# Attention ahead of a gated FFN: the queries of the first eight steps without their zeros, scored head by head on tiles of 64 rows by 32 columns, in a new order of all work

## The chip, the cores and the metric

The kernel runs on one core of a Trainium2 chip. The metric is the device time of one execution in microseconds (us); lower is better. Before the change it was 360.17 us, the median of three runs (359.59, 360.17 and 361.05).

## What is computed

Four batches, eight heads, 768 positions, 64 elements a head. The positions are cut into 24 chunks of 32. A chunk's queries see 16 positions to the left, their own 32, 8 to the right, and 8 memory positions that each head has of its own. The result goes through a feed-forward layer with a convolution over three positions and a sigmoid gate:

```
for c in range(nc):                                   # 24 chunks of 32 positions
    k_full = concat(mem_k, k[l_start:r_end])          # 8 memory + up to 56 positions
    scores = 1/sqrt(64) * q_c @ k_full.T
    a = exp(scores - max(scores));  a = a / (sum(a) + 1e-09)
    out[c] = a @ v_full
x = out, heads side by side                           # 4 x 768 x 512
h = relu(x @ w_in)                                    # 512 -> 1024
conv = w[0] * h[t-1] + w[1] * h[t] + w[2] * h[t+1]
y = (h * sigmoid(conv)) @ w_out                       # 1024 -> 512
```

All inputs are float32 except the three weights of the FFN, which are float64.

## The kernel before

**Steps.** Attention is cut into 32 steps. A step is one batch, one half of the positions (`hf`, 12 chunks) and one pair of heads (`cc`, 0 to 3). A step loads three tiles through SyncE's queue: the queries `q_d` (128 partitions by 12 x 64, 384 KB), the keys and memory keys `k_t` (128 by 504, 252 KB) and the values `v_t` (128 by 768, 384 KB). Steps 0 to 3 keep queries and keys in buffers named `h`, steps 4 to 7 in buffers named `g`, which the FFN uses later; the others use two buffers each of `q_d` and `k_t`.

In `q_d` the partitions are 2 heads x 64 elements. For each chunk there are 64 columns: the first 32 hold head 0's queries in partitions 0 to 63 and zeros below, the last 32 hold head 1's queries in partitions 64 to 127 and zeros above (`_laid_out` writes this on the host as it lays the inputs out). So half of what is loaded is zeros, and one matmul with all 128 rows gives the scores of both heads of a chunk.

**Scores (`scores`, L476 to L490).** Twelve matmuls, one for each chunk, each 64 queries by 64 keys, in the two column halves of the array (`j`). All land in one PSUM bank `s` (a ring of two banks). The trace shows two records for each such float32 matmul, 24 for a step.

**Softmax.** VectorE takes the maximum (L398), subtracts it (L403), ScalarE takes the exponential (L436); or ScalarE does both from PSUM (L424) with the maximum as its bias, with (`B`) or without (`A`) the sums. Then sums (L449), 1e-9 (L453), reciprocal (L456) and the product (L460) on VectorE or GpSimd. The strings `SOFT`, `ZADD` and `NORM` choose engine and form for each step.

**Outcome.** Three transposes on TensorE (L506), two copies to `a_d` on ScalarE (L517), twelve matmuls with the values (L525), then `x_hi` on ScalarE (L534) and `x_lo` on VectorE (L537): two parts of the attention output for the FFN. Transposes and values share a ring of two PSUM banks, `ta`.

**FFN.** `w_in` and `w_out` come as float64 and are split into a high and a low part by `from_f64`; the letters of `W_IN` and `W_OUT` choose the engines of the eight pieces of each (`c` and `C` use ScalarE and GpSimd for some operations, `R` and `S` use GpSimd for three or two, `M` nearly only VectorE; a small letter puts L294 on GpSimd). `ffn_in` (L560) takes twelve matmuls of 384 columns for a piece of 128 hidden channels and half the positions; `gate` and `split` do convolution, sigmoid and product on VectorE, ScalarE and GpSimd (`TAP`, `MULT`, `LO`); `ffn_out` (L636) takes 24 matmuls for 128 positions.

**Order.** Nothing is scheduled by hand. `Plan` takes every operation with an engine, a cost and a due time, and places them in one list: on each engine the ready operation with the smallest due time is next. `DUE` holds the due times as start and step of a line for each stage, `SWITCH` and `MODE` are added to the due time where ScalarE's table or TensorE's tiling would change. The list sets the order of the instructions of every engine and of the DMA queue. On the chip the engines wait for each other by semaphores only.

Of the kernel before, what the change touches and what calls it, by code (L numbers as in the profile page):

```python
# [19 lines left out]
CH, LEFT, RIGHT, NMEM = 32, 16, 8, 8  # L20
KW = LEFT + CH + RIGHT + NMEM
STEP = CH + NMEM
NH = 2
NC = 12
NG = NC // 4
KC = STEP * (NC - 1) + KW

TINY = 1.75 * 2.0**-15
W64 = 3
WC = 512  # L30


W_IN, W_OUT = "ccRRMMcR", "CCCsSRmm"

TAP = "AAAAAAAAAVAVVVVVVAAAAAVAAVVAAAVA"
MULT = "GGGGGGGGGGGGGVVGGGVVGGGGGGGVGVGG"
LO = "VVVGGGGGGGVVVGVVVVVVVVGGGGGGGVVG"
SOFT = "VVAVVVVVVVVVVVAABBVVVVVVBBVVVVBB"  # L40
NORM = "GGGGGGGGGGGGGGVGGGGVGVGVVVVVGGGV"
ZADD = "VGGGGVGGGVGVVGGGVVVVGGGVVVVGVVVV"
GROUP = "11111111"

DUE = {
    "early": (1.5, 1.76), "qk0": (-11, 1.21), "v0": (46.7, 0), "late": (-4.7, 0.51), "w_in": (-21.5, 2.2),
    "w_in_load": (-23.8, 6.98), "w_out": (61.7, 2.41), "w_out_load": (18.4, 7.34), "load": (-167, 1.78),
# [4 lines left out]
    "gate": (1.2, 6.13)  # L52
}
# [9 lines left out]
class Plan:  # L63
# [47 lines left out]
    def run(self):  # L111
        ops = self.ops
        n = len(ops)
# [21 lines left out]
        for _ in range(n):  # L135
# [34 lines left out]
            t, e, i = best  # L170
            eng, cost, due, do, after, tiles, shared, tab, md, late = ops[i]
# [3 lines left out]
            if md and md != mode:  # L175
                cost += 95 if md == "tiled" else 200
                mode = md
# [35 lines left out]
PAIRS = False  # L213
SWITCH, MODE = 102.0, 16.4


@with_exitstack
def attention_then_gated_ffn(
    ctx: ExitStack,
    tc: tile.TileContext,  # L220
    q: bass.AP,
    k: bass.AP,
# [150 lines left out]
    def attention(steps, due, soft, norm, zadd):  # L373
# [9 lines left out]
        for i, n in enumerate(steps):  # L383
            b, r = divmod(n, NU)
            cc = r % NCC

            q_d, k_t = (tile_of(*(("h", NFC) if n < 4 else ("g", 2 * NFC) if n < 8 else (x, 2)), y) for x, y in (("q_d", [P, NC, 2 * CH]), ("k_t", [P, KC])))
            v_of[n] = v_t = tile_of("v_t", 3, [P, NG, 2, 2, D])
            s = bank("s", 2)
            qk, vd = (lin("qk0", n), lin("v0", n)) if n < 8 else (due[i] - DUE["load"][0], due[i] - DUE["load"][0] + DUE["load"][1])  # L390
            load(q_d, q[b, hf, cc], qk, "p c q -> p (c q)")
            load(k_t, k[b, hf, cc], qk)
            load(v_t, v[b, hf, cc], vd, "p g c h d -> p (g c h d)")
            scores(s, q_d, k_t, due[i])
            s_ = lambda s=s: s.t[:, :W].rearrange("p (g k) -> p g k", k=KW)
# [79 lines left out]
    def scores(s, q_d, k_t, due):  # L475
# [257 lines left out]
def _laid_out(q, k, v, mem_k, mem_v):  # L733
# [22 lines left out]
    for h in range(2):  # L756
        ql[:, :, :, h, :, :, h] = qt[:, :, :, h]
    ql = ql.reshape(B, NH, H // 2, 2 * D, NC * 2 * CH)
    w = windows(k, mem_k).reshape(B, H // 2, 2, NH, NC, KW, D)
    kl = np.empty((B, H // 2, 2, NH, KC, D), k.dtype)  # L760
# [4 lines left out]
    vl = w.transpose(0, 3, 1, 6, 7, 4, 5, 2, 8).reshape(B, NH, H // 2, 2 * KW, NG * 4 * D)  # L765
    return [np.ascontiguousarray(a) for a in (ql, kl, vl)]

# [39 lines left out]
```

## Time and profile before

| | |
|---|---|
| median of three runs | 360.17 us |
| the profiled execution's own time | 359.69 us |
| its span, first to last instruction | 357.8 us |
| VectorE busy | 248.4 us (69%) |
| ScalarE busy | 231.6 us (65%) |
| GpSimd busy | 152.5 us (43%) |
| moved by DMA | 48.62 MB |

The span is what the profile's times refer to; 1.9 us of the execution lie around it. Engines are named PE (TensorE's matmuls), PEld (its weight loads, which overlap the matmuls), DVE (VectorE), ACT (ScalarE), POOL (GpSimd) and SP (SyncE, which only issues DMAs). A line of a timeline gives start, duration, engine, source line, the operation with what it writes and reads, the number of instructions, and in brackets the idle time of the engine before it with what ended it.

### The profile page before, as it was taken

Reading aid. Unit: us, or ns where it says so; the run is one execution under the profiler, and the core shown is the slowest. Engines: PE = TensorE matmul, PEld = TensorE weight load, DVE = VectorE, ACT = ScalarE, POOL = GpSimd, SP = SyncE. Lnnn points to the kernel's source line nnn. Section 1 sums busy time; section 2 is a strip of 40 time slices with the busy share of each in tenths; the row PEclk is TensorE's granted clock in tenths of the full one; section 3 lists DMA queues with packets and bytes.
Section 4 is the critical chain, followed back from the end, with each engine's and each line's share of the span. In section 5 each row is a group of like instructions: output and inputs, shape, how many; then the busy total and the mean of one; then the engine's idle time right before and its main releaser. Section 6 shows DMA issues by size and latency. Waiting matters only on the chain.

```text
span 357.8 us, 7562 instructions
## 1 busy us (share of the span) xinstructions
PE 339.2 (95%) x3000; PEld 301.3 (84%) x3000; DVE 248.4 (69%) x401; ACT 231.6 (65%) x457; POOL 152.5 (43%) x180
## 2 busy tenths in 40 slices
PE   1789999999999998998999999999999999999996
PEld 1678898989999876876888899999878799998886
DVE  2798998999999699998994026998503137998000
ACT  3568777579898898769734137999837345764201
POOL 5356616544783589676321003015721005783200
PEclk9999999999999999999999999999999999999999
DMA  7999892768451047480401200461312100000111
GB/s 286 401 393 330 279 333 82 276 209 266 163 177 61 0 147 235 163 289 35 178 2 59 88 31 0 147 235 27 136 64 71 61 29 2 0 0 2 59 59 60
DMA packets 19907, 48.62 MB, mean 136 GB/s; under 512 B 2336, under 2 KB 6688, under 8 KB 19872
## 3 DMA queue, kind: packets, MB, share of 16 engines
q1 hardware_dynamic: 19872, 48.14, 38.4%
q8 instruction: 24, 0.39, 0.5%
q14 instruction: 11, 0.09, 0.1%
HBM read 41.84 MB, written 6.29 MB: 135 GB/s over the span
## 4 chain that ended last, share of the span: by engine, by line
PE 61%; DVE 20%; DMA 8%; ACT 5%; issue 3%; POOL 2%; SPq 0%; ACTq 0%
PE f L636 29%; PE f L560 26%; PE ta L525 3%; DVE c L597 2%; DVE w_top L307 2%; DVE z L449 2%; DMA v_t<-in_v_dram 2%; DMA g<-in_q_dram 2%; PE s L482 2%; DVE x_lo L537 2%; DMA h<-in_k_dram 2%; DVE w L328 1%; DVE w_top L300 1%; DMA w<-in_w_in_dram 1%; DVE w L321 1%
## 5 line engine op out<-in xcount | busy, mean ns | idle before, releaser
L636 PE MATMUL f<-w_out_hi,g 128*128 128x512 f32 (+1 forms) x400 | 126.6, 390 | 0.0
L560 PE MATMUL f<-x_hi,w_in_hi 128*128 128x384 f32 x256 | 88.2, 344 | 0.0
L636 PEld LDWEIGHTS f<-w_out_hi,g 128*128 128x128 f32 x400 | 74.0, 188 | 16.5 <-POOL g L618 0.4
L560 PE MATMUL f<-x_lo,w_in_hi 128*128 128x384 f32 x256 | 86.3, 337 | 0.6 <-DVE x_lo L537 0.6
L560 PE MATMUL f<-x_hi,w_in_lo 128*128 128x384 f32 x256 | 86.1, 336 | 0.0
L636 PE MATMUL f<-w_out_lo,g 128*128 128x512 f32 (+1 forms) x200 | 77.1, 386 | 0.0
L597 DVE SCALAR_TENSOR_TENSOR c<-h,cw,c 128x768 f32<-128x768 f32 x48 | 66.9, 1399 | 11.3 <-ACT c L587 9.6
L560 PEld LDWEIGHTS f<-x_hi,w_in_hi 128*128 128x128 f32 x256 | 48.1, 188 | 1.1 <-ACT g L577 0.3
L560 PEld LDWEIGHTS f<-x_lo,w_in_hi 128*128 128x128 f32 x256 | 48.1, 188 | 1.1 <-DVE x_lo L537 1.1
L560 PEld LDWEIGHTS f<-x_hi,w_in_lo 128*128 128x128 f32 x256 | 48.2, 188 | 0.2
L605 POOL TENSOR_TENSOR c<-c,h 128x768 f32<-128x768 f32 x12 | 21.4, 1785 | 61.7 <-ACT c L601 61.6
L636 PEld LDWEIGHTS f<-w_out_lo,g 128*128 128x128 f32 x200 | 37.6, 188 | 7.2
L648 ACT COPY o_sb<-f 128x512 f32<-128x512 f32 (+1 forms) x25 | 14.0, 569 | 40.9 <-PE f L636 33.6
L460 POOL TENSOR_TENSOR e<-e,z 128x384 f32<-128x384 f32 x23 | 22.7, 988 | 32.1 <-DVE e L444 12.9
L577 ACT ACTIVATE h<-f 128x384 f32<-128x384 f32 x48 | 23.1, 491 | 19.3 <-PE f L560 19.0
L517 ACT COPY a_d<-ta 64x384 f32<-64x384 f32 x64 | 30.2, 472 | 7.2 <-PE ta L506 6.4
L601 ACT ACTIVATE c<-c 128x768 f32<-128x768 f32 x32 | 26.9, 846 | 9.5 <-DVE c L597 7.2
L537 DVE TENSOR_TENSOR x_lo<-ta,x_hi 128x384 fp32r<-128x384 f32 x32 | 16.9, 545 | 22.6 <-ACT x_hi L534 22.2
L618 POOL TENSOR_TENSOR g<-c,g 128x768 fp32r<-128x768 f32 x13 | 28.6, 2213 | 7.9 <-ACT g L615 7.9
L525 PEld LDWEIGHTS ta<-a_d,v_t 128*64 128x64 f32 x768 | 24.4, 138 | 5.6 <-issue 2.8
L525 PE MATMUL ta<-a_d,v_t 128*64 128x64 f32 x768 | 27.3, 224 | 1.3 <-DMA v_t<-in_v_dram 1.2
L615 ACT CAST g<-c 128x768 fp32r<-128x768 f32 x24 | 19.9, 828 | 6.4 <-POOL c L605 4.9
(76 smaller groups left out, 488.4 us busy)
## 6 DMA issues: line engine op xcount, KB each, us to landing
v_t<-in_v_dram SPq DMA_DIRECT2D x32, 384.0 KB, 4.7
q_d<-in_q_dram SPq DMA_DIRECT2D x24, 384.0 KB, 4.8
k_t<-in_k_dram SPq DMA_DIRECT2D x24, 252.0 KB, 4.9
out_dram<-o_sb SPq DMA_DIRECT2D x23, 256.0 KB, 2.0
w<-in_w_in_dram SPq DMA_DIRECT2D x8, 512.0 KB, 5.1
w<-in_w_out_dram SPq DMA_DIRECT2D x8, 512.0 KB, 3.9
h<-in_q_dram SPq DMA_DIRECT2D x4, 384.0 KB, 7.2
g<-in_q_dram SPq DMA_DIRECT2D x4, 384.0 KB, 6.6
```

What stands on the lines that cost most here:

```text
L460: lambda i=i: (nc.vector if norm == "V" else nc.gpsimd).tensor_tensor(out=part(e, i), in0=part(e, i), in1=part(z, i).unsqueeze(2).broadcas ...
L517: nc.scalar.copy(out=a_d[r, :, p, :], in_=t.t[r, : NG * P].rearrange("p (g q) -> p g q", q=CH))
L525: nc.tensor.matmul(a.t[h * D : (h + 1) * D, g * P + j * D : g * P + (j + 1) * D], lhsT=v_t.t[:, g, j, h], rhs=a_d[:, 4 * g + 2 * j + h].re ...
L537: lambda: nc.vector.tensor_tensor(out=x_lo.t[:, cc], in0=a.t[:, :TW], in1=x_hi.t[:, cc].bitcast(F32), op=ALU.subtract),
L560: nc.tensor.matmul(f.t[:, :TW], lhsT=w_in_p[c][:, fc, cc], rhs=x_p[a].t[:, cc], start=(cc == 0 and i == 0), stop=(cc == NCC - 1 and i == 2),)
L577: nc.scalar.activation(h.t[:, 1 + o : 1 + o + TW], f.t[:, :TW], AF.Relu)
L597: lambda i=i: nc.vector.scalar_tensor_tensor(out=c.t, in0=h.t[:, i : i + S], scalar=w[i], in1=c.t, op0=ALU.mult, op1=ALU.add), (*H, c), (c ...
L601: plan.op("A", act(S), due, lambda: nc.scalar.activation(c.t, c.t, AF.Sigmoid), (c,), (c,), table="sigmoid")
L605: lambda: (nc.vector if mult == "V" else nc.gpsimd).tensor_tensor(out=y(), in0=c.t, in1=h.t[:, 1 : S + 1], op=ALU.mult), (c, h), (h if kee ...
L615: plan.op("A", act(S), due, lambda: nc.scalar.copy(out=g_hi(), in_=x()), (h,), (p[0],))
L618: lambda: (nc.vector if lo == "V" else nc.gpsimd).tensor_tensor(out=g_lo(), in0=x(), in1=g_hi().bitcast(F32), op=ALU.subtract), (h, p[0]), ...
L636: nc.tensor.matmul(ps.t[:, :n], lhsT=g[fc][a].t[:, tt * P : (tt + 1) * P], rhs=w_out_p[c][:, fc, o : o + n], start=(fc == 0 and i == 0), s ...
```

## The change

A new input `q_first` holds the queries of the first eight steps without zeros: 128 partitions (2 heads x 64) by 12 chunks x 32 queries, 192 KB a step in place of 384 KB. Their scores are taken by a new function, `scores_apart`: for each chunk and head one matmul with the 64 rows of that head and 32 columns, so 24 matmuls for a step in place of 12. The four that follow each other (`j`, `h`) go to the four 32-partition quarters of the same PSUM bank, and what they write is what `scores` wrote. The planner counts them as a third tiling mode. Steps 8 to 31 keep their form.

The letters of all engine strings, all due times, `SWITCH` and `MODE`, and the planner's cost for a change of tiling are new as well; `SOFT` for instance gives step 2 the form `B` in place of `A`.

```diff
+NQ = 8
-W_IN, W_OUT = "ccRRMMcR", "CCCsSRmm"
+W_IN, W_OUT = "SRRRSCRC", "sSCsRRRm"
-MULT = "GGGGGGGGGGGGGVVGGGVVGGGGGGGVGVGG"
+MULT = "GGGGGVVVVGGVGVVVVGGVVVVGGGGGGVVV"
...
-    "early": (1.5, 1.76), "qk0": (-11, 1.21), "v0": (46.7, 0), "late": (-4.7, 0.51), "w_in": (-21.5, 2.2),
+    "early": (1.5, 3.25), "qk0": (-19.9, 1.15), "v0": (21.1, 0), "late": (-15.5, 0.53), "w_in": (-7.3, 2.44),
...
-                cost += 95 if md == "tiled" else 200
+                cost += 95 if mode == "whole" else 200 if md == "whole" else 140
...
-("q_d", [P, NC, 2 * CH])
+("q_d", [P, NC, CH if n < NQ else 2 * CH])
-            load(q_d, q[b, hf, cc], qk, "p c q -> p (c q)")
+            load(q_d, q_first[n] if n < NQ else q[b, hf, cc], qk, "p c q -> p (c q)")
-            scores(s, q_d, k_t, due[i])
+            (scores_apart if n < NQ else scores)(s, q_d, k_t, due[i])
...
+    def scores_apart(s, q_d, k_t, due):
+        def mm():
+            for g in range(NG):
+                for p in range(2):
+                    for j in range(2):
+                        for h in range(2):
+                            c, r, o = 4 * g + 2 * j + p, slice(h * D, (h + 1) * D), (2 * g + p) * KW
+                            nc.tensor.matmul(
+                                s.t[j * D + h * CH : j * D + (h + 1) * CH, o : o + KW],
+                                lhsT=q_d.t[r, c],
+                                rhs=k_t.t[r, c * STEP : c * STEP + KW],
+                                start=True,
+                                stop=True,
+                            )
+        plan.op("PE", 48 * 16, due, mm, (q_d, k_t), (s,), mode="rows", late=250)
```

**TensorE, from its first matmul to the first matmul of the FFN.** Before (`s` are scores, `ta` transposes and values; twelve matmuls are one step's scores or values, three are one step's transposes):

```order
L482 MATMUL s<-h 64x64 x48
L506 MATMUL ta<-ident,e 128x128 x3
L482 MATMUL s<-g 64x64 x12
L506 MATMUL ta<-ident,e 128x128 x3
L482 MATMUL s<-g 64x64 x24
L525 MATMUL ta<-a_d_71,v_t 64x64 x12
L525 MATMUL ta<-a_d_72,v_t 64x64 x12
L560 MATMUL f<-x_hi_337,w_in_hi 128x384
```

The same place in the changed kernel, where 24 matmuls of 32 by 64 are one step's scores (L503), L527 the transposes, L546 the values and L581 the FFN:

```order
L503 MATMUL s<-h 32x64 x96
L527 MATMUL ta<-ident,e 128x128 x6
L503 MATMUL s<-g 32x64 x48
L546 MATMUL ta<-a_d_71,v_t 64x64 x12
L503 MATMUL s<-g 32x64 x24
L546 MATMUL ta<-a_d_72,v_t 64x64 x12
L581 MATMUL f<-x_hi_406,w_in_hi 128x384
```

Both transposes now stand ahead of step 4's scores, and step 6's scores stand between the two groups of values. Seven steps' scores are ahead of the FFN in both.

**SyncE's DMA queue, from its start.** Before:

```order
L287 DMA w_82<-in_w_in_dram 128x1024
L287 DMA w_84<-in_w_in_dram 128x1024
L472 DMA h<-in_q_dram 128x768
L472 DMA h<-in_k_dram 128x504
L287 DMA w_90<-in_w_in_dram 128x1024
L472 DMA h<-in_q_dram 128x768
```

and now:

```order
L289 DMA w_82<-in_w_in_dram 128x1024
L474 DMA h<-in_q_first_dram 128x384
L474 DMA h<-in_k_dram 128x504
L474 DMA h<-in_q_first_dram 128x384
L474 DMA h<-in_k_dram 128x504
L474 DMA h<-in_q_first_dram 128x384
```

One piece of `w_in` (512 KB) is ahead of step 0 in place of two. The second now stands behind step 3's keys and the third behind step 7's; then come three `v_t` in both kernels.

**VectorE, from its start to the reciprocal of step 0.** Before, with two pieces of `w_in` (`w_82`, `w_84`) between the steps' operations:

```order
L316 TENSOR_SCALAR w_82<-w_82 128x512
L321 SCALAR_TENSOR_TENSOR w_82<-w_82 128x512
L316 TENSOR_SCALAR w_84<-w_84 128x512
L300 TENSOR_SCALAR w_top<-w_top 128x512
L398 TENSOR_REDUCE top<-s 128x6
L403 TENSOR_TENSOR e<-s,top 128x384
L307 SCALAR_TENSOR_TENSOR w_top<-w_82,w_top 128x512
L328 TENSOR_SCALAR w_82<-w_top 128x512
```

and now:

```order
L296 TENSOR_SCALAR w_top<-w_top 128x512
L302 TENSOR_SCALAR w_top<-w_top 128x512
L309 SCALAR_TENSOR_TENSOR w_top<-w_82,w_top 128x512
L330 TENSOR_SCALAR w_82<-w_top 128x512
L400 TENSOR_REDUCE top<-s 128x6
L405 TENSOR_TENSOR e<-s,top 128x384
L400 TENSOR_REDUCE top<-s 128x6
L405 TENSOR_TENSOR e<-s,top 128x384
L343 SCALAR_TENSOR_TENSOR w_82<-w_82 128x512
```

Steps 0 and 1 have their maximum and difference one behind the other, and one operation on the weights stands between them and step 2's.

More of the change, by code (lines that the diff above doesn't have):

```diff
@@ L28 @@
 TINY = 1.75 * 2.0**-15
+NQ = 8
 W64 = 3
 WC = 512
-W_IN, W_OUT = "ccRRMMcR", "CCCsSRmm"
-TAP = "AAAAAAAAAVAVVVVVVAAAAAVAAVVAAAVA"
-MULT = "GGGGGGGGGGGGGVVGGGVVGGGGGGGVGVGG"
[L39 to L42, printed above, removed]
+W_IN, W_OUT = "SRRRSCRC", "sSCsRRRm"
+TAP = "AAAAAAAAVAVAAVAAVVAAAAAAAVAAVAVV"
+MULT = "GGGGGVVVVGGVGVVVVGGVVVVGGGGGGVVV"
+LO = "VGVGVGGGVGVGVVVVVGVVGGGGGVVGGVVV"
+SOFT = "VVBVVVVVBVVVVVAABBVVVVVVVVVAAVAV"
+NORM = "GGVGGGGGGGGGGGGVGGVVGGVVGGGGVGGG"
+ZADD = "VGGGGVGGVVVVGGGGGVGGGGVVGVVGGVVV"
 GROUP = "11111111"
 DUE = {
-    "early": (1.5, 1.76), "qk0": (-11, 1.21), "v0": (46.7, 0), "late": (-4.7, 0.51), "w_in": (-21.5, 2.2),
-    "w_in_load": (-23.8, 6.98), "w_out": (61.7, 2.41), "w_out_load": (18.4, 7.34), "load": (-167, 1.78),
[4 rows of a table removed]
-    "gate": (1.2, 6.13)
+    "early": (1.5, 3.25), "qk0": (-19.9, 1.15), "v0": (21.1, 0), "late": (-15.5, 0.53), "w_in": (-7.3, 2.44),
+    "w_in_load": (-23.6, 7.37), "w_out": (60.9, 2.74), "w_out_load": (25.4, 4.97), "load": (-219.2, 1.82),
[4 rows of a table added]
+    "gate": (-4.6, 9.82)
 }
@@ L213 @@
 PAIRS = False
-SWITCH, MODE = 102.0, 16.4
+SWITCH, MODE = 98.4, 24.0
 @with_exitstack
@@ L220, in attention_then_gated_ffn @@
     tc: tile.TileContext,
+    q_first: bass.AP,
     q: bass.AP,
@@ L385, in attention @@
             cc = r % NCC
-            q_d, k_t = (tile_of(*(("h", NFC) if n < 4 else ("g", 2 * NFC) if n < 8 else (x, 2)), y) for x, y in (("q_d", [P, NC, 2 * CH]), ("k_t", [P, KC])))
+            q_d, k_t = (tile_of(*(("h", NFC) if n < 4 else ("g", 2 * NFC) if n < 8 else (x, 2)), y) for x, y in (("q_d", [P, NC, CH if n < NQ else 2 * CH]), ("k_t", [P, KC])))
             v_of[n] = v_t = tile_of("v_t", 3, [P, NG, 2, 2, D])
@@ L758, in _laid_out @@
     ql = ql.reshape(B, NH, H // 2, 2 * D, NC * 2 * CH)
+    qf = qt.reshape(B * NH * (H // 2), 2 * D, NC * CH)[:NQ]
     w = windows(k, mem_k).reshape(B, H // 2, 2, NH, NC, KW, D)
@@ L765, in _laid_out @@
     vl = w.transpose(0, 3, 1, 6, 7, 4, 5, 2, 8).reshape(B, NH, H // 2, 2 * KW, NG * 4 * D)
-    return [np.ascontiguousarray(a) for a in (ql, kl, vl)]
+    return [np.ascontiguousarray(a) for a in (qf, ql, kl, vl)]
 def _words(a):
@@ L784 @@
     B, H, S, D = q.shape
-    ql, kl, vl = _laid_out(*(_np.asarray(a) for a in (q, k, v, mem_k, mem_v)))
+    qf, ql, kl, vl = _laid_out(*(_np.asarray(a) for a in (q, k, v, mem_k, mem_v)))
     ins = {
+        "q_first": qf,
         "q": ql,
```

8 rows, old and new, of the table DUE are left out of this document.

## The prediction

> **What bounds the kernel.** First the page's first part, then busy time by stretch, then TensorE's waits, then its timeline.
>
> ```profile
> PE 339.2 (95%) x3000; PEld 301.3 (84%) x3000; DVE 248.4 (69%) x401; ACT 231.6 (65%) x457; POOL 152.5 (43%) x180
> ```
>
> ```profile
> 0.00:25.00 25.00, 13.91 (x225) 12.26 (x226) 16.07 (x41) 12.73 (x25) 12.71 (x20) 1.00 0.95 359
> 25.00:50.00 25.00, 24.40 (x357) 22.22 (x356) 23.58 (x56) 18.33 (x40) 13.16 (x22) 1.00 0.91 314
> 50.00:100.00 50.00, 48.72 (x475) 45.50 (x474) 47.89 (x90) 39.62 (x82) 27.35 (x46) 1.00 0.61 203
> ```
>
> The first row is the page's, the others are the windows'; their columns are stretch, length, then busy time of PE, PEld, DVE, ACT and POOL, the granted clock, DMA's share and GB/s. PE idles 11 us of the first 25, when DMA is 95% busy, and 1.9 us of the next 75. DVE is the second engine: 94 to 96% busy from 25 to 100 us. What can be gained lies in the start and in PE's waits:
>
> ```profile
> PE s L482 <- DMA h<-in_k_dram: 9.2, 2, 7.8
> PE ta L506 <- DVE x_lo L537: 1.5, 4, 0.9
> PE ta L506 <- DVE e L460: 1.3, 1, 1.3
> PE ta L525 <- DMA v_t<-in_v_dram: 1.2, 1, 1.2
> PE ta L506 <- POOL e L460: 0.7, 3, 0.3
> PE f L560 <- DVE x_lo L537: 0.6, 1, 0.6
> ```
>
> Columns: total us, times, longest. Ahead of the FFN PE waits for DMA; behind it the waits are 1.5 + 1.3 + 0.7 + 0.6 = 4.1 us. The start in PE's timeline:
>
> ```profile
> 7.82 1.55 PE L482 MATMUL s<-h 128*64 128x64 f32 x24 [7.82 <-DMA h<-in_k_dram]
> ...
> 15.95 0.90 PE L506 MATMUL ta<-ident,e 128*128 128x128 f32 x3
> 16.78 1.55 PE L482 MATMUL s<-g 128*64 128x64 f32 x24
> 18.26 0.90 PE L506 MATMUL ta<-ident,e 128*128 128x128 f32 x3
> 19.09 2.24 PE L482 MATMUL s<-g 128*64 128x64 f32 x48
> 22.54 1.90 PE L525 MATMUL ta<-a_d,v_t 128*64 128x64 f32 x48 [1.21 <-DMA v_t<-in_v_dram]
> 24.37 0.44 PE L560 MATMUL f<-x_hi,w_in_hi 128*128 128x384 f32 x1
> 24.65 0.34 PE L560 MATMUL f<-x_hi,w_in_lo 128*128 128x384 f32 x1
> ...
> 26.92 0.34 PE L560 MATMUL f<-x_lo,w_in_hi 128*128 128x384 f32 x1
> 27.19 0.92 PE L525 MATMUL ta<-a_d,v_t 128*64 128x64 f32 x24
> 27.94 0.87 PE L482 MATMUL s<-g 128*64 128x64 f32 x24
> 28.64 0.87 PE L482 MATMUL s<-k_t,q_d 128*64 128x64 f32 x24
> 29.34 0.87 PE L525 MATMUL ta<-a_d,v_t 128*64 128x64 f32 x24
> 30.14 0.55 PE L506 MATMUL ta<-ident,e 128*128 128x128 f32 x3
> ...
> 33.01 0.52 PE L506 MATMUL ta<-ident,e 128*128 128x128 f32 x3 [0.23 <-DVE x_lo L537]
> 33.29 0.42 PE L560 MATMUL f<-x_hi,w_in_hi 128*128 128x384 f32 x1
> ```
>
> The first FFN matmul stands at 24.37 us; from there PE works without a long gap, so how early that matmul starts is the first term. One step's 24 score records take 1.55 us at 16.78 and 0.87 at 27.94, though every stretch reads clock 1.00: TensorE is slow at the start and turns fast inside the 48 records of 19.09 (2.24 us lies between two slow and two fast groups).
>
> **What half the queries save in DMA.** SP issues one DMA each time an older one has landed:
>
> ```profile
> 7.70 0.33 SPq L472 DMA_DIRECT2D g<-in_q_dram  x1
> 8.98 0.33 SPq L472 DMA_DIRECT2D g<-in_k_dram  x1
> 9.98 0.33 SPq L472 DMA_DIRECT2D g<-in_q_dram  x1
> 10.63 0.33 SPq L472 DMA_DIRECT2D g<-in_k_dram  x1
> ```
>
> ```profile
> 14.89 7.52 DMA v_t<-in_v_dram
> ```
>
> The distances are those of landings: 1.28 us for a piece of `w_in` (512 KB), 1.00 for queries (384 KB), 0.65 for keys (252 KB); all are some 400 GB/s. The last row, of the chain of waits in order of time, says that the first `v_t` landed at 22.41. Queries of 192 KB would take 0.49 us at that rate; the shorter runs of 1.5 KB a partition aren't in the trace, and can hardly take longer than the keys' 0.65, which are more bytes. I take 0.53, near the rate. So 8 x 0.46 = 3.7 us are saved (2.7 to 4.0) and the first `v_t` lands near 18.7. Step 0's keys have one piece of `w_in` and half the queries less ahead of them: 1.28 + 0.46 = 1.75 us, so the first score matmul moves from 7.82 to about 6.0.
>
> **The path from there to the FFN** is no longer DMA's. Its rows:
>
> ```profile
> 9.40 0.56 DVE L398 TENSOR_REDUCE top<-s 128x6 f32<-128x384 f32 x1 [1.63 <-PE s L482]
> 10.47 0.68 DVE L307 SCALAR_TENSOR_TENSOR w_top<-w,w_top 128x512 uint32<-128x512 uint32 x1
> 14.08 0.83 POOL L460 TENSOR_TENSOR e<-e,z 128x384 f32<-128x384 f32 x1 [1.16 <-DVE z L456]
> 29.87 1.28 POOL L352 TENSOR_TENSOR w_in_lo<-w_top,w_in_hi 128x512 fp32r<-128x512 f32 x1
> ```
>
> By the new order of DVE: scores of step 0 at 6.0 to 7.5; maximum and difference of step 0 and of step 1 (four rows of about 0.58 with their start) to 10.2 with the wait for step 1's scores; one weight operation (0.7) to 10.9; step 2's maximum 11.5; step 0's sums, addition and reciprocal 12.5; POOL's product 13.4; so the first transposes at about 13.5, 7.5 us behind the scores where it was 8.1. The second wait for POOL, which has an addition, a `w_in_lo` (1.28) and a product (0.83) to do: about 16.1, and 17.0 at their end. Then steps 4 and 5 at 1.4 each (16.78 to 18.26 is 1.48 with the switch), and the first values at 19.9: behind `v_t`, so that the 1.2 us wait for DMA goes and PE's own program is late next. Behind it stand step 6's scores (0.7) in the 1.83 us that lay between 22.54 and 24.37. **First FFN matmul at 19.9 + 0.7 + 1.8 = 22.4, 2.0 us earlier.** If only `v_t` bounded, 18.7 + 2.5 = 21.2, 3.1 us earlier.
>
> **What a step's scores cost apart.** The trace has no 64x32 matmul, so the cost is bounded by its rows. Three fast transposes of 128 moving columns each start within 0.28 us (33.01 to 33.29), some 0.1 us each, 0.8 ns a column. At that pace a score record of 64 columns would take 50 ns, yet 24 take 0.70 us (27.94 to 28.64), 29 ns each. So I read them as running two at a time, in the two column halves. A step now has 48 such records in four quarters. Four at a time gives 48 x 14.6 ns = 0.70 us fast and about 1.4 slow, as now; two at a time twice that, 1.4 and 2.8. Below nothing is excluded: each record streams as many columns as before. I take four at a time: the four consecutive matmuls use disjoint rows or columns of the array, as those do that overlap now.
>
> A rule speaks against it. The Trainium skill, "TensorEngine Tiling (Array Packing)", Gotcha 1 (PSUM Pressure), says that different row tiles cannot access one PSUM bank at the same time; here both row halves write one bank, in different partitions. No run here shows it yet. By that rule it is two at a time, the case of the first two rivals.
>
> **The order behind it.** Each change between whole and tiled matmuls costs PE time: 26.92 to 27.19 is 0.27 where L560's pitch is 0.17, 29.34 to 30.14 is 0.80 where a group takes 0.70, and 24.37 to 24.65 is 0.28; together 0.3 us for a turn and back. Counted in the orders behind the first FFN matmul there are 21 such turns before and 24 now: **+0.9 us** (none, if they fall into waits). The FFN, transposes and values are as many, and the last 306 FFN matmuls stand as they did, so the tail stays.
>
> DVE is what could stop PE from being early. The largest edits to it in the first 200 us:
>
> ```profile
> L321 DVE SCALAR_TENSOR_TENSOR w<-w 128x512 uint32<-128x512 uint32 x10 | 7.6, 756 | 0.1
> L316 DVE TENSOR_SCALAR w<-w 128x512 uint32<-128x512 uint32 x10 | 5.7, 573 | 4.5 <-DMA w<-in_w_in_dram 4.4
> L605 DVE TENSOR_TENSOR c<-c,h 128x768 f32<-128x768 f32 x4 | 3.8, 950 | 0.0
> ```
>
> The new `W_IN` and `W_OUT` take six of each of the first two (6 x 1.33 = -8.0) and add about 2 in three others of 0.6 to 0.7 each; the first 16 letters of `MULT` put six more products on DVE (6 x 0.95 = +5.7) and take them off POOL. So DVE has about as much to do as before. Its rows also stand earlier against PE's: before, PE waits for DVE's `x_lo` and `e` in 3.4 of the 4.1 us; with fewer of the weight pieces' DVE rows ahead of those waits I let 2.5 of the 4.1 us go: **-2.5 us** (from all gone, -4.1, to 1.5 of new waits, since PE also asks 2 us earlier). POOL gets operations like L352's 1.28 us for the further `R` pieces and gives up ten products; with 57% of its span idle I cost this at nothing, and where it is late after all, that is in the upper end of these waits. ScalarE's (35% idle) too.
>
> **Sum:** -2.0 + 0.9 - 2.5 = -3.6 us against the profiled execution's own 359.69 (its span 357.8 and 1.9 around it): 356.1. That execution is 0.5 under the median of the runs, so 356.6. Its own range: -3.1 to -1.0 for the start, 0 to 0.9 for the turns and -4.1 to +1.5 for the waits give 353.0 to 361.6.
>
> **Rivals.**
> 1. *Two at a time, TensorE soon fast.* With 2.6 to 2.8 us a step at first PE has no gap from 6.0 on. Slow records end here after some 4 us of unbroken work (16.78 to about 20.3), so say from 11 us on a step takes 1.4. Then by the same path the first transposes stand at about 15.3, the second at 17.9, steps 4 and 5 end at 21.3, and values, step 6 (1.4) and values put the FFN at 24.5: +0.1, and +0.7 for step 7 behind it: 357.8 + 0.1 + 0.7 + 0.9 - 2.5 + 1.9 + 0.5 = 359.4.
> 2. *Two at a time, slow throughout the start:* slower than before. PE is then the bound of the start: scores of four steps from 6.0 to 16.4, two transposes to 18.8, two steps to 24.2, values 1.4, step 6 2.7, values 1.4: the FFN at 29.7, 5.3 us later: 357.8 + 5.3 + 0.7 + 0.9 - 2.5 + 2.4 = 364.6. It decides once the FFN starts behind 25.3 (24.4 + 2.5 - 0.9 - 0.7); with seven steps ahead of it that takes about 2.0 us a step in place of 2.6. For it: rows of 1.55 us a step fill most of PE's start already. Against it: the fast rows from 20.3 on, after unbroken work. The Trainium skill, "TensorE: Matmul & The Clock Gate", Part 1, says that the array runs at half its clock until a window of about 3.4 us was busy; the doubling of the rows agrees, the clock column of this profile doesn't show it. By that rule this rival ends at the first one's time.
> 3. *No saving:* short runs take as long as long ones, 1.0 us, so that loads pace the start as before and only order remains: the 1.28 us of `w_in` at step 0 don't count at `v_t`, FFN at 24.4 + 0.7: 357.8 + 0.7 + 0.9 - 2.5 + 2.4 = 359.3. Against it: keys and queries land in proportion to their bytes.
>
> **Chances:** the forecast 0.57, rival 1 0.24, rival 2 0.11, rival 3 0.08. A measurement of this kernel can tell about 0.5% (1.8 us) from no change. The forecast is faster by more than that in nine cases of ten, rivals 1 and 3 in three of ten: 0.61 faster. Half of rivals 1 and 3 and the forecast's upper end give 0.21 the same; rival 2 and the upper ends of the others 0.18 slower. The range goes from 353.0, the forecast's lower end, to 362.0, which takes in rival 1 with none of the 2.5 us gained (361.9); rival 2 is left out.
>
> **What would show it.** Right: step 0's scores near 6.0 us, one step's 48 records in about 1.4 slow and 0.7 fast, first FFN matmul near 22.4, PE's waits behind it near 1.6 us. Wrong: a step's records in 2.8 or 1.4, `v_t` still last ahead of the first values, or waits for DVE behind 25 us above 4 us, which would mean that the earlier start is given back.

## The result and the profile after

The changed kernel takes 361.77 us (median of 20 runs, 360.52 to 365.01), the kernel before 360.03 (20 runs, 359.32 to 362.21). The ratio is 1.0051, with a 95% interval of 1.0031 to 1.0071: slower by half a per cent, where 356.6 had been forecast. The profiled execution of the changed kernel took 363.55 us (span 361.7), 1.8 above its median; that of before took 359.69. Of the 20 executions, the ten with a mean granted clock of 0.989 or more have a median of 361.1 us, and the ten of 0.986 or less, the profiled one (0.985) among them, 363.1.

The page's first row and the busy time by stretch, as they were shown of before (stretch, length, busy PE, PEld, DVE, ACT, POOL, granted clock, DMA's share, GB/s):

```profile
PE 340.7 (94%) x3192; PEld 301.9 (83%) x3192; DVE 252.8 (70%) x398; ACT 230.8 (64%) x443; POOL 146.6 (41%) x183
```

```profile
0.00:25.00 25.00, 12.85 (x388) 11.06 (x390) 15.52 (x37) 11.84 (x31) 11.76 (x20) 0.83 0.95 345
25.00:50.00 25.00, 24.03 (x358) 21.83 (x356) 22.03 (x55) 17.26 (x47) 13.05 (x21) 0.97 0.75 240
50.00:100.00 50.00, 47.52 (x444) 44.08 (x443) 46.35 (x79) 38.54 (x78) 33.13 (x47) 1.00 0.61 194
```

PE does 192 matmuls and 192 weight loads more, and is busy 1.1 us less in the first 25 us, 0.4 less in the next 25 and 1.2 less in the 50 behind. Its timeline at the start (start, us, engine, line, operation, count, and in brackets the idle time ahead and what ended it):

```profile
5.90 4.02 PE L503 MATMUL s<-h 64*32 64x64 f32 x144 [5.90 <-DMA h<-in_k_dram]
10.18 0.87 PE L503 MATMUL s<-h 64*32 64x64 f32 x48 [0.26 <-DVE e L405]
13.36 0.90 PE L527 MATMUL ta<-ident,e 128*128 128x128 f32 x3 [2.31 <-POOL e L462]
16.00 0.90 PE L527 MATMUL ta<-ident,e 128*128 128x128 f32 x3 [1.74 <-POOL e L462]
16.83 2.79 PE L503 MATMUL s<-g 64*32 64x64 f32 x96
19.55 0.97 PE L546 MATMUL ta<-a_d,v_t 128*64 128x64 f32 x24
20.45 0.64 PE L503 MATMUL s<-g 64*32 64x64 f32 x28
23.03 0.82 PE L503 MATMUL s<-g 64*32 64x64 f32 x20 [1.95 <-issue]
23.78 1.55 PE L546 MATMUL ta<-a_d,v_t 128*64 128x64 f32 x24
25.26 0.69 PE L581 MATMUL f<-x_hi,w_in_hi 128*128 128x384 f32 x1
```

Up to 20.45 every row stands within 0.4 us of the forecast. Then PE stops in the middle of step 6's scores, behind 28 of 48 matmul records, for 1.95 us, and the releaser is "issue": nothing that the profile shows. The values behind run slow (1.55 us), and the first FFN matmul comes at 25.26, not 22.4. The slow rows stand where the granted clock is low; the windows' view in three shorter stretches:

```profile
12.88:19.70 6.82, 4.60 (x104) 3.70 (x106) 5.27 (x14) 5.11 (x20) 5.31 (x7) 0.50 1.04 398
19.70:23.12 3.42, 1.47 (x57) 1.24 (x61) 2.85 (x8) 1.97 (x4) 1.50 (x3) 1.00 1.05 384
23.12:26.53 3.41, 3.41 (x48) 3.03 (x49) 1.12 (x2) 0.48 (x1) 1.23 (x3) 0.50 0.65 234
```

In the stretch that holds the stop, PE was busy 1.47 us of 3.42; in the next 3.41 us the clock column reads 0.50 again.

Behind the start PE's waits are not fewer. Some rows of the view (line that waits, what for, total us, times, longest):

```profile
PE s L503 <- issue: 1.9, 1, 1.9
PE f L581 <- DVE x_lo L558: 1.4, 1, 1.4
PE ta L527 <- DVE x_lo L558: 1.1, 3, 0.6
PE f L657 <- ACT o_sb L669: 1.0, 1, 1.0
PE ta L546 <- ACT a_d L538: 0.8, 2, 0.4
PE s L484 <- DMA k_t<-in_k_dram: 0.6, 1, 0.6
```

Below the first of these rows, which is the stop in the start, and with two of 0.3 and 0.2, they come to 5.4 us behind the first FFN matmul, where 4.1 stood before and 1.6 were forecast. From the first FFN matmul to PE's last it takes 329.8 us before (24.37 to 354.19) and 332.9 after (25.26 to 358.13). So 0.9 us are lost ahead of the first FFN matmul and 3.1 behind it. Some 0.6 of the 3.1 is still the half clock: the first three FFN matmuls and the three transposes behind them take 1.45 us here, up to 26.70, and 0.87 at full clock in the third experiment below.

Two theories for the start follow. One: PE waits for its own instructions. The trace has an instruction queue (q8 on the page's list of DMA queues); its packets of 16,384 bytes and their times are read from the packed trace. One such transfer began at 20.39, and PE stood still once it had begun 705 records (matmuls and weight loads counted together), so that the 706th came late. Each matmul of 64 rows by 32 columns leaves two matmul records and two weight loads, so a step apart has 96 records where it had 48. The Trainium skill, "Runtime: NRT & Kernel Launch", "Instruction fetch mechanics", says that instructions are refilled in blocks of 16 KiB, 256 instructions, while the block before runs, and that this is mostly hidden; the size of the packets agrees, and by this theory 1.95 us of it are not hidden here. The rival: something in step 6 itself, its bank, operands or the clock.

### The profile page after: what moved, and what is told of

It is laid out like the page before. It is cut to its first block, busy times and chain, and to the rows that moved or that the text cites. A ratio compares the mean times of both kernels' runs of the same rounds, so it can differ in the third digit from the quotient of the medians.

```text
span 361.7 us, 7932 instructions
## 1 busy us (share of the span) xinstructions
PE 340.7 (94%) x3192; PEld 301.9 (83%) x3192; DVE 252.8 (70%) x398; ACT 230.8 (64%) x443; POOL 146.6 (41%) x183
## 4 chain that ended last, share of the span: by engine, by line
PE 72%; DVE 9%; DMA 7%; ACT 5%; POOL 4%; issue 2%; SPq 1%; ACTq 0%; POOLq 0%; DVEq 0%
PE f L657 33%; PE f L581 26%; PE ta L546 5%; PE s L484 3%; DMA w<-in_w_in_dram 3%; PE ta L527 2%; PE s L503 2%; DMA out_dram<-o_sb 2%; DMA k_t<-in_k_dram 1%; POOL e L462 1%; DMA h<-in_k_dram 1%; DVE w_top L309 1%; ACT o_sb L669 1%; DVE w L318 1%; DVE w L343 1%
## 5 line engine op out<-in xcount | busy, mean ns | idle before, releaser
L581 PE MATMUL f<-x_hi,w_in_hi 128*128 128x384 f32 x256 | 88.6, 346 | 0.3 <-ACT g L598 0.2
L581 PE MATMUL f<-x_lo,w_in_hi 128*128 128x384 f32 x256 | 86.5, 338 | 1.4 <-DVE x_lo L558 1.4
L581 PE MATMUL f<-x_hi,w_in_lo 128*128 128x384 f32 x256 | 86.4, 337 | 0.3 <-POOL w_in_lo L354 0.3
L618 DVE SCALAR_TENSOR_TENSOR c<-h,cw,c 128x768 f32<-128x768 f32 x48 | 63.5, 1333 | 25.1 <-ACT c L608 23.8
L581 PEld LDWEIGHTS f<-x_lo,w_in_hi 128*128 128x128 f32 x256 | 48.3, 189 | 2.0 <-DVE x_lo L558 2.0
L581 PEld LDWEIGHTS f<-x_hi,w_in_hi 128*128 128x128 f32 x256 | 48.2, 188 | 1.6 <-ACT g L598 0.6
L581 PEld LDWEIGHTS f<-x_hi,w_in_lo 128*128 128x128 f32 x256 | 48.3, 189 | 0.7 <-POOL w_in_lo L354 0.6
L626 POOL TENSOR_TENSOR c<-c,h 128x768 f32<-128x768 f32 x8 | 14.1, 1757 | 66.3 <-ACT c L622 66.3
L462 POOL TENSOR_TENSOR e<-e,z 128x384 f32<-128x384 f32 x25 | 25.3, 1017 | 36.7 <-DVE z L458 20.0
L639 POOL TENSOR_TENSOR g<-c,g 128x768 fp32r<-128x768 f32 x13 | 26.3, 2026 | 10.4 <-ACT g L636 10.4
L546 PEld LDWEIGHTS ta<-a_d,v_t 128*64 128x64 f32 x768 | 25.0, 141 | 6.0 <-issue 2.9
L546 PE MATMUL ta<-a_d,v_t 128*64 128x64 f32 x768 | 28.1, 228 | 0.8 <-ACT a_d L538 0.8
L400 DVE TENSOR_REDUCE top<-s 128x6 f32<-128x384 f32 x32 | 17.6, 549 | 8.3 <-PE s L484 5.7
```

Source lines behind the costliest of these rows:

```text
L400: lambda i=i, s_=s_: nc.vector.tensor_reduce(out=part(top, i), in_=s_(), axis=AX.X, op=ALU.max), (s,), ((top, i),),
L462: lambda i=i: (nc.vector if norm == "V" else nc.gpsimd).tensor_tensor(out=part(e, i), in0=part(e, i), in1=part(z, i).unsqueeze(2).broadcas ...
L546: nc.tensor.matmul(a.t[h * D : (h + 1) * D, g * P + j * D : g * P + (j + 1) * D], lhsT=v_t.t[:, g, j, h], rhs=a_d[:, 4 * g + 2 * j + h].re ...
L581: nc.tensor.matmul(f.t[:, :TW], lhsT=w_in_p[c][:, fc, cc], rhs=x_p[a].t[:, cc], start=(cc == 0 and i == 0), stop=(cc == NCC - 1 and i == 2),)
L618: lambda i=i: nc.vector.scalar_tensor_tensor(out=c.t, in0=h.t[:, i : i + S], scalar=w[i], in1=c.t, op0=ALU.mult, op1=ALU.add), (*H, c), (c ...
L639: lambda: (nc.vector if lo == "V" else nc.gpsimd).tensor_tensor(out=g_lo(), in0=x(), in1=g_hi().bitcast(F32), op=ALU.subtract), (h, p[0]), ...
```

## The experiments

Where a kernel keeps another's order, the planner's costs, due times and modes were left as they were and only what is done at each place was changed, so that DVE, ACT, POOL and PE keep their sequence. The cuts of code leave out the arguments that do this. "The new order" stands for all that was re-made with it: due times, costs and the letters that choose engines.

**The order without the apart scores.** All eight steps load padded queries and use 24-record scores:

```diff
-            load(q_d, q_first[n] if n < NQ else q[b, hf, cc], qk, "p c q -> p (c q)")
+            load(q_d, q[b, hf, cc], qk, "p c q -> p (c q)")
-            (scores_apart if n < NQ else scores)(s, q_d, k_t, due[i])
+            scores(s, q_d, k_t, due[i])
```

> The new order with the old scores: the eight first steps load their zero-padded queries (393 KB in place of 197 KB) and take 24 matmuls a step; every engine's and SP's order is that of the changed kernel. Theory (the order was to be worth some 2.5 us behind the first FFN matmul, and the changed kernel lost its gain in a stall of 1.95 us inside step 6's scores): no stall in step 6, first v_t lands 3.7 us later than in the changed kernel, at 22.8, first FFN matmul 25.0 to 25.8, time 361 to 362.5, the same as the changed kernel, since the stall and the slow clock had eaten what the smaller loads saved. Rival (the order itself loses 3 us behind the first FFN matmul and the apart scores gained at the start): from the first FFN matmul to PE's last 332.9 as in the changed kernel and the time 363 or more. Second rival (a stall in step 6 that comes from the order and not from the apart scores): step 6's scores again stop for about 2 us, time above 364.

363.21 us, ratio 1.0087 [1.0062, 1.0112]. PE's timeline:

```profile
22.26 1.55 PE L547 MATMUL ta<-a_d,v_t 128*64 128x64 f32 x24 [1.05 <-DMA v_t<-in_v_dram]
23.57 1.52 PE L485 MATMUL s<-g 128*64 128x64 f32 x24
24.85 1.52 PE L547 MATMUL ta<-a_d,v_t 128*64 128x64 f32 x24
26.30 0.67 PE L582 MATMUL f<-x_hi,w_in_hi 128*128 128x384 f32 x1
```

No stop in step 6, so the order does not make it. But the re-made order alone costs 0.9%: step 6's scores now lie behind the late `v_t`, and the clock is low there:

```profile
16.57:26.81 10.24, 8.21 (x125) 7.60 (x126) 6.86 (x17) 6.12 (x17) 5.26 (x7) 0.50 1.04 397
```

The first FFN matmul stands at 26.30, 1.9 us later than before and later than the theory's 25.0 to 25.8, and from there it takes 331.3 us against 329.8. The time is the first rival's (363 or more), its 3 us behind the first FFN matmul are 1.5.

**The apart scores without the order.** The old tables and the old sequence on every engine, with small loads and `scores_apart` for all eight steps.

```diff
-            load(q_d, q[b, hf, cc], qk, "p c q -> p (c q)")
+            load(q_d, q_first[n] if n < NQ else q[b, hf, cc], qk, "p c q -> p (c q)")
-            scores(s, q_d, k_t, due[i])
+            (scores_apart if n < NQ else scores)(s, q_d, k_t, due[i])
```

> The small loads and the apart scores alone, in the order of the kernel before on every engine. Theory (small loads bring the first v_t 3.7 us earlier; a pause for instruction loading some 56 PE records behind record 649 of PE falls here into the first values): first v_t lands near 18.7, a stall of 0.5 to 1.5 us inside the first values, first FFN matmul 21.0 to 22.3 against 24.37 before, from there to the end 329.8 as before, time 356.5 to 358.5. Rival (what the start gains is lost behind it, because the work behind the first FFN matmul waits for loads and conversions that come no earlier): first FFN matmul 21 to 22 but the time 359.5 or more. Second rival (apart scores cost more in this order): first FFN matmul not before 23.5, time 359.5 or more.

361.7 us, ratio 1.0035 [1.0012, 1.0057]. PE's timeline:

```profile
15.80 0.87 PE L503 MATMUL s<-g 64*32 64x64 f32 x24
17.24 0.87 PE L503 MATMUL s<-g 64*32 64x64 f32 x24 [0.57 <-issue]
...
21.34 0.34 PE L546 MATMUL ta<-a_d,v_t 128*64 128x64 f32 x4
23.51 1.89 PE L546 MATMUL ta<-a_d,v_t 128*64 128x64 f32 x44 [1.84 <-issue]
```

PE stops twice for "issue", once in step 4 and once in the first values, after 449 and 705 records. The second is the count of the changed kernel, at another place of the program and another kind of matmul. The place was as the theory said; the size (1.84), a second stop and the first FFN matmul (25.33, not 21.0 to 22.3) were not, and the time missed its 356.5 to 358.5. By its numbers the second rival holds: eight steps apart cost more in this order too, by the stops. From the first FFN matmul on it takes 330.7 us.

**Steps 4 to 7 the old way, in the new order.** As the first experiment, but steps 0 to 3 stay apart.

```diff
+APART = range(4)
-            (scores_apart if n < NQ else scores)(s, q_d, k_t, due[i])
+            (scores_apart if n in APART else scores)(s, q_d, k_t, due[i])
```

> The changed kernel with steps 4 to 7 done the old way (padded queries, 24 matmuls a step), steps 0 to 3 apart, the order of every engine held. PE then has executed 192 records fewer by the end of step 7. Theory (the stall in step 6 is PE waiting for instructions, one load for 256 records, and too many small matmuls in too short a time): no stall in step 6 or anywhere up to the first FFN matmul; the first v_t lands 1.9 us later than in the changed kernel (0.79 MB more ahead of it), at 21.0; first FFN matmul 22.7 to 23.5 in place of 25.26; time 359 to 360.3, 1.5 to 2.8 below the changed kernel. Rival (the stall has another cause at this place of the program, a semaphore or the clock's change): it stays at step 6, about 2 us, first FFN matmul at 26 to 27, time 362.5 or more.

361.12 us, ratio 1.0028 [1.0005, 1.0051]. PE's timeline:

```profile
20.83 0.92 PE L547 MATMUL ta<-a_d,v_t 128*64 128x64 f32 x24 [1.16 <-DMA v_t<-in_v_dram]
21.55 0.90 PE L485 MATMUL s<-g 128*64 128x64 f32 x24
22.25 0.90 PE L547 MATMUL ta<-a_d,v_t 128*64 128x64 f32 x24
23.08 0.44 PE L582 MATMUL f<-x_hi,w_in_hi 128*128 128x384 f32 x1
```

The start did as the theory said: no stop, first FFN matmul at 23.08, 1.3 us earlier than before. The time did not follow (359 to 360.3 had been expected): behind it 332.8 us, as in the changed kernel. So the new order loses time behind the start even where PE never stops for "issue".

**Idle matmuls ahead of the scores.** 64 matmuls of 64x32 on the identity, into a bank not yet used, which nothing reads:

```diff
+    idle = psum.tile([P, 512], F32, name="f", tag="f", bufs=4)
+    for i in range(64):
+        j, h = i // 2 % 2, i % 2
+        r = slice(h * D, (h + 1) * D)
+        nc.tensor.matmul(
+            idle[j * D + h * CH : j * D + (h + 1) * CH, :KW], lhsT=ident[r, :CH], rhs=ident[r, :KW], start=True, stop=True
+        )
```

> The changed kernel with 64 idle matmuls of 64 rows by 32 columns (128 PE records) on the identity, into a bank that is not yet in use, ahead of the first scores, while PE has nothing else to do; no other order changes and nothing reads them. Theory (instruction loading every 256 records, with a lead of 56 records): the transfer of 16 KB that started at record 649 of PE comes at about the same count of records, so 128 records earlier in the program, in step 5's scores, and the stall moves from step 6's 29th matmul to the end of step 5; step 6 runs through; first FFN matmul 23.2 to 24.8, time 359.8 to 361.3. Rival (the stall belongs to step 6, its bank, its operands or the clock): it stays behind the 28th matmul of step 6 and first FFN matmul at 25.0 to 25.5, time 361.8.

362.4 us, ratio 1.0061 [1.0035, 1.0086]. The 64 matmuls left 256 records, not the 128 of the expectation, a whole period by the theory:

```profile
20.94 1.00 PE L511 MATMUL s<-g 64*32 64x64 f32 x28
22.86 0.53 PE L511 MATMUL s<-g 64*32 64x64 f32 x20 [0.92 <-issue]
```

The stop stays behind step 6's 28th record, now with 961 records begun, 256 more. Both theories allow that, so this run does not decide. With 32 idle matmuls the shift is 128:

> The run before with 64 idle matmuls had moved the count of PE's records by 256 (each matmul is two matmul records and two weight loads), one whole period, and the stall stood at record 962, 256 behind the 706 of the changed kernel. Here 32 idle matmuls, 128 records. Theory (PE's instructions come in blocks of 256, and a block is asked for when 56 are left): the stall is at record 706 again, which is now the 73rd of the 96 records of step 5's scores; step 6 runs through without a stop, the next one would be at 962, behind the first FFN matmul where 56 records last longer than the transfer; transfer to resumption 2.4 to 2.7 us. First FFN matmul 23.3 to 24.5, time 360.5 to 362. Rival (the stall belongs to step 6 or to what lies near it in time): it is again after step 6's 28th matmul.

360.2 us, ratio 1.0003 [0.9977, 1.0028]. PE's timeline:

```profile
6.59 4.73 PE L511 MATMUL s<-h 64*32 64x64 f32 x156 [3.31 <-DMA h<-in_k_dram]
12.91 1.28 PE L511 MATMUL s<-h 64*32 64x64 f32 x36 [1.59 <-issue]
...
21.82 1.19 PE L511 MATMUL s<-g 64*32 64x64 f32 x48
...
23.79 0.45 PE L589 MATMUL f<-x_hi,w_in_hi 128*128 128x384 f32 x1
```

Step 6 runs through, and the rival is out. A stop stands after 449 records, in step 3. None stands after 705, in step 5, which the theory had wanted: PE went on behind the 449 at 12.91, the transfer for the next block began at 15.01, in the wait for the second transposes, and PE came to the 705 only at 19.78. So the request does not go out a fixed 56 records ahead. Five stops, by the transfers of 16,384 bytes and PE's count, fit another rule: a block of 256 is asked for about when the one before it begins. ("Old order, 8" is the second experiment; "256 shifted" and "128 shifted" are the runs with 64 and 32 idle matmuls.)

```
kernel         stop after   block ahead   transfer    PE goes   from the block
               records      begins at     starts at   on at     ahead to there
changed           705         17.36         20.39      23.03         5.67
old order, 8      449         10.96         14.63      17.24         6.28
old order, 8      705         17.24         21.07      23.51         6.27
256 shifted       961         17.29         20.30      22.86         5.57
128 shifted       449          7.34         10.35      12.91         5.57
```

PE goes on 2.4 to 2.6 us behind the start of each transfer, and the transfer starts 3.0 to 3.8 us after the block ahead began. In these five PE had to wait 5.6 to 6.3 us for its next 256 records. Steps 4 and 5, the values and step 6 up to the stop use up a block in 3.5 (17.36 to 20.87). The rule is one of these stops, not of the whole kernel: later, where matmuls are long, transfers start up to 4.9 us ahead of the record that it names (in the kernel before; 3.7 in the changed kernel, at 343.49), and the trace does not tell when a block is asked for.

**Four steps apart in the old order.** The second experiment with `NQ = 4`: half of the small loads, and fewer records.

> The order of the kernel before on every engine; steps 0 to 3 alone with small loads and apart, steps 4 to 7 the old way. By the count of records the block that ends at 449 falls into the wait for the second transposes and that at 706 behind the first FFN matmul, so no stall is seen at either. Theory (the start gains if no instruction stall and no re-made order takes it back): first v_t lands 1.9 us earlier than before, at 20.5; first FFN matmul 22.4 to 23.2 against 24.37; behind it 329.8 to 330.3; time 358.3 to 359.5, a ratio of 0.994 to 0.998. Rival (work behind the start sets the end, so that an earlier first FFN matmul only waits longer later): first FFN matmul as said, but 331 or more behind it and the time 360 to 361, a ratio of 1.000 or above.

357.34 us (357.0 to 358.2), ratio 0.9914 [0.9886, 0.9943]: faster than before and than the changed kernel, and below the 358.3 to 359.5 expected.

```profile
17.40 0.25 PEld L527 LDWEIGHTS ta<-ident,e 128*128 128x128 f32 x2 [0.84 <-issue]
17.81 1.91 PE L484 MATMUL s<-g 128*64 128x64 f32 x48
20.96 1.90 PE L546 MATMUL ta<-a_d,v_t 128*64 128x64 f32 x48 [1.23 <-DMA v_t<-in_v_dram]
22.78 0.44 PE L581 MATMUL f<-x_hi,w_in_hi 128*128 128x384 f32 x1
```

The first FFN matmul is 1.6 us earlier than before, and 330.0 us stand behind it: the start's gain is kept. PE stops here too: inside the second transposes, again after 449 records, it goes on at 17.40, 2.37 us behind a transfer that began at 15.03. (GpSimd had finished the product that these transposes read at 16.24.) This costs nothing, because the first values wait for `v_t` until 20.96. Against the third experiment, with the same four steps apart and the first FFN matmul within 0.3 us, only the order (with its letters) differs: 332.8 us behind it and 1.0028 there, 330.0 and 0.9914 here, with intervals far apart. The profiled execution, the slowest of six, gains 1.5 us on that of before (359.69 to 358.2); the profiles do not show where the rest of the medians' 3.1 comes from.

**Idle matmuls for the clock.** The same with four long ones, whose output nothing reads: 2 x 512 columns ahead of the scores, 256 behind the first transposes and 256 behind step 4's scores:

```diff
+    def warm(i, n):
+        nc.tensor.matmul(idle[:, :n], lhsT=ident, rhs=a_ds[i].rearrange("p g c q -> p (g c q)")[:, :n], start=True, stop=True)
```

> As the run with four steps apart in the old order, with four long idle matmuls on zeros and the identity (two of 512 columns ahead of the first scores, one of 256 behind the first transposes, one of 256 behind step 4's scores), whose output nothing reads. Theory (part of the loss at the start is the half clock of PE, in windows of 3.413 us, when the first values run): the granted clock is full from about 17 on in place of 20 to 21, first values 0.7 to 1.0 us a step in place of 1.5, first FFN matmul 0.5 to 1.5 us earlier than without the idle matmuls, time 0.3 to 1.5 us lower. Rival (windows do not follow four matmuls, or the first values wait for v_t and not for the clock): first FFN matmul within 0.3 us, time the same within the interval.

357.95 us, ratio 0.9931 [0.9905, 0.9957]; no gain, the rival is right. The first values still wait for their load, and the first FFN matmul is at 23.05:

```profile
21.24 1.89 PE L558 MATMUL ta<-a_d,v_t 128*64 128x64 f32 x48 [0.98 <-DMA v_t<-in_v_dram]
```

**Half of the order.** The third experiment with the eight tables of letters of before under the new due times and costs.

```diff
-MULT = "GGGGGVVVVGGVGVVVVGGVVVVGGGGGGVVV"
+MULT = "GGGGGGGGGGGGGVVGGGVVGGGGGGGVGVGG"
...
```

> Steps 0 to 3 apart and 4 to 7 the old way as in the run before of that kind, with the new due times, switch and mode costs, but the tables of letters (which engine does which conversion, tap, product, low part, softmax) of the kernel before. Theory (the 2 us of new waits behind the first FFN matmul come from the due times, which put transposes, scores and values elsewhere on PE): the sum of PE's waits over 0.25 us behind the first FFN matmul stays at 7 us or more, time 360.5 to 362.5. Rival (they come from the letters, which give DVE or ACT work at the wrong moment): the sum falls to below 6 us and the time to 358 to 360.

367.5 us, ratio 1.0204 [1.0168, 1.0239], outside both. The old letters under the new due times are slower than either order whole, so the loss can't be shared out between them in this way.

**Five steps apart in the old order** (`NQ = 5`).

> As the run with steps 0 to 3 apart in the old order, with step 4 apart as well: 0.2 MB less ahead of the first v_t, 48 matmul and 48 weight-load records fewer to spare. Theory (a block of 256 records is asked for when the one before it begins and is there 5.6 to 6.4 us later): record 449 now lies in the middle of step 4's scores and PE stops there until about 17.3; first v_t lands at 20.5; record 705, asked for at 17.3 and there at 22.9 to 23.7, lies six or seven matmuls behind the first FFN matmul, which comes at 22.2 to 22.6; a stall there of 0 to 0.8 us. What the smaller load gains (0.4) is about what the stalls cost: time 356.8 to 358, the same as with four steps. Rival (small loads pay whatever the blocks do): no stall, 356.3 to 356.9. Second rival (every step apart costs): 358.2 or more.

359.26 us, ratio 0.9981 [0.9963, 1.0]: the second rival's time (358.2 or more).

```profile
17.78 0.87 PE L503 MATMUL s<-g 64*32 64x64 f32 x24 [0.57 <-issue]
18.57 0.90 PE L527 MATMUL ta<-ident,e 128*128 128x128 f32 x3
19.40 2.83 PE L484 MATMUL s<-g 128*64 128x64 f32 x48
22.02 1.95 PE L546 MATMUL ta<-a_d,v_t 128*64 128x64 f32 x48
```

The stop in step 4 is where the block rule put it, after 449 records, 6.3 us behind the 193. I had priced it against the smaller load. But the second transposes, queued behind it on PE, come 1.2 us later than with four steps (0.6 of it since the first scores, at 7.85 and 7.21 us), steps 5 and 6 take 2.83 in place of 1.91, and the values no longer wait for `v_t`: the first FFN matmul stands at 23.90. In this execution one more step apart turns a bound by loads into one by PE.

**The first `v_t` ahead of step 7's loads.** Four steps apart in the old order; SP issues step 7's queries and keys behind the second `v_t`; the other engines' order stays. In SP's order:

```diff
-v_t of step 0, v_t of step 1
 g <- queries and keys of step 7
+v_t of step 0, v_t of step 1 (ahead of these two)
```

> As the run with steps 0 to 3 apart in the old order, but step 7's query and keys (0.65 MB) load behind the first two v_t in place of ahead of them; no other engine's order changes. Theory (the start is bound by the landing of the first v_t, then by step 6's scores): first v_t lands 1.5 us earlier, at 19.4; first values at 19.7 to 19.9 when step 6's scores end; first FFN matmul 21.4 to 22.0 against 22.78; behind it 330 to 331; time 355.9 to 357.0. Rival (the work behind waits for conversions and loads that come no earlier, so an earlier first FFN matmul waits longer there): 331 or more behind it and the time 357 to 358.

356.87 us (355.82 to 357.57), ratio 0.9917 [0.9895, 0.994], the lowest median.

```profile
20.28 1.57 PE L553 MATMUL ta<-a_d,v_t 128*64 128x64 f32 x48
21.78 0.44 PE L588 MATMUL f<-x_hi,w_in_hi 128*128 128x384 f32 x1
```

The first FFN matmul stands at 21.78, as the theory said, and 330.1 us behind it. The ratio can't be told from that of four steps alone. Here too PE stops after 449 records, for 0.28 us until 17.46.

**Instruction blocks where DMA is idle.** Four steps apart in the old order, and 256 idle 64x32 matmuls behind the last FFN matmul, whose output nothing reads.

> As the run with steps 0 to 3 apart in the old order, with 256 idle matmuls of 64 rows by 32 columns (1024 PE records) behind the last FFN matmul, where the DMA queues are nearly empty; they add work that nothing reads. Theory (a block of 256 PE records is there a latency behind the moment at which it is asked for, and what makes 5.6 to 6.4 us of it in the start is the load on the DMA queues): PE stops once in 256 records, some 2 us of records and a stop, with 3 to 4.5 us from one stop's end to the next. Rival (the latency is fixed): 5.6 to 6.4 us from one stop's end to the next. Second rival (the stops in the start are no instruction loading): the 1024 records run through in some 8 us.

One run, 366.67 us. PE's timeline at the end:

```profile
351.59 2.42 PE L756 MATMUL s<-ident 64*32 64x64 f32 x154
355.14 1.99 PE L756 MATMUL s<-ident 64*32 64x64 f32 x128 [1.14 <-issue]
358.87 1.99 PE L756 MATMUL s<-ident 64*32 64x64 f32 x128 [1.74 <-issue]
362.33 1.65 PE L756 MATMUL s<-ident 64*32 64x64 f32 x102 [1.46 <-issue]
```

PE stops every 128 matmul records (256 with the weight loads), and goes on 3.73 and 3.46 us after it last went on. The transfers began at 352.70, 356.18 and 359.96, so the last two 1.0 and 1.1 us after PE went on with a block, and all 2.4 to 2.7 ahead of PE's going on. The latter is what it was in the start; the former was 3.0 to 3.8 at the five stops there. Both rivals are out, and the theory's 3 to 4.5 us from stop to stop hold. That the load on DMA makes the difference is not shown: DMA was 95% busy in the first 25 us and is 7% here, but in the changed kernel a transfer began only 1.8 us after PE went on (23.03 to 24.86), with DMA 98% busy.

## Why the prediction was wrong

*The saving in DMA, the first scores and the path to the first values* were right: first score matmul 5.90 (6.0 forecast), transposes 13.36 and 16.00 (13.5, 16.1), first `v_t` landed at 19.11 (18.7), first values 19.55 (19.9), no wait for `v_t` ahead of them.

*Four at a time* was right: where the clock column reads 0.50, two steps take 2.79 us (16.83), 1.4 each, and at full clock a step's row is 0.87 (10.18), that of before. Rivals 1 and 2 did not come about. The Trainium skill's Gotcha 1 (PSUM Pressure, "TensorEngine Tiling (Array Packing)") says that different row tiles cannot access one PSUM bank at the same time; no cost of that is visible in these rows. The prediction's clock readings of 1.00 for the start of before rest on no record: the trace of before holds no clock record ahead of 20.32 us, and the view counts what has no record as full.

*"Behind it stand step 6's scores (0.7) in the 1.83 us"* is the first step that failed. It counted what 48 matmul records cost the array, and put at nothing that a step apart issues 96 records (weight loads with them) in place of 48. The stop of 1.95 us and the half clock behind it put the first FFN matmul at 25.26 in place of 22.4, so the start's -2.0 became +0.9. That it is instructions that PE waits for was shown: the stop keeps its count (449, 705, 961), not its place, it goes when records go or are shifted, and 1024 extra records make one stop in 256. That the half clock follows from the stop is likely and not shown; in the second experiment too the clock reads 0.50 from 24.43 on, behind the stop that ended at 23.51.

*Turns, +0.9 us.* What PE takes from the first FFN matmul on, less its waits over 0.25 us (counted as in the next paragraph), grows by 0.0 (order alone) to 0.7 us (256 shifted) in the new order, and by 0.9 in the changed kernel, 0.6 of it the half clock. The term was rather too high.

*"I let 2.5 of the 4.1 us go"* is the second step that failed, and the larger. The two longest waits of before, 0.93 and 1.30 us ahead of transposes at 139.67 and 168.12, did go; the new order brought others, for `x_lo` ahead of an FFN matmul (1.4), `o_sb` (1.0), `a_d` (0.8) and keys (0.6). In place of 1.6 the view has 5.4 us. It tells a wait from the modelled end of the matmul ahead. Counted from start to start, less what a matmul of that kind takes in a row, the waits over 0.25 us sum to 5.6 before, 7.7 in the changed kernel, 6.1 to 7.9 in the five kernels with the whole new order, and 4.4 to 6.0 in the five old-order kernels in which steps were apart and nothing was added at the end. DVE was busy 83.9 us in the first 100, against 87.5 before, and the waits came all the same. I had looked at which waits of the old order the new one relieves, and charged none of its own beyond +1.5 at the range's edge. An earlier start need not be given back: from the first FFN matmul on, the old order with four or five steps apart takes 329.0 to 330.1 us (329.8 before), the new order 330.8 to 332.9. Why the new order waits more, which of its rows sit badly, stays open; one half of it by itself was no help.

*The sum.* Forecast were -2.0 + 0.9 - 2.5; the profiled execution shows +0.9 at the first FFN matmul and +3.1 behind it, together the 3.9 us by which it is over that of before (363.55 and 359.69). By medians it is 1.7, and how these share out between start and waits one profiled execution does not show. The forecast's own range ended at 361.6; the time lies inside the whole range only because that was widened to 362.0 for rival 1, which did not come about. That is luck.

## What to carry to other kernels

Price an edit that splits matmuls by instructions too, not by array time alone: count PE's records (weight loads with them) along the start, and look whether 256 of them are wanted in less time than a block took to come, here 5.6 to 6.4 us at the stops in the start and 3.5 to 3.7 at the end. A stop only costs where nothing else is later, as the one in the kernel with four steps shows. A re-made order has waits of its own, so test a change and the order that came with it apart: here the change, in four of eight steps, gained 0.9% in the old order, and with the new one was 0.3% slower than before.

## What the runs showed of the hardware

PE can run out of instructions: at the stops in the start, the 16 KB packet for the next block starts 3.0 to 4.1 us after PE begins the block ahead, and at the end of the kernel, with DMA 7% busy, 1.0 to 1.1 us after; PE goes on 2.4 to 2.7 us behind the packet's start in both. A stop can cost twice: in the changed kernel a window of 3.42 us in which PE was busy 1.47 was followed by one at half the granted clock, in which the values behind the stop took 1.55 us in place of 0.97.
